# Head products, reciprocal transposes and first scaling half a unit apart at each batch's end, in a fused attention and mixture-of-experts kernel

## The chip, the cores and the metric

The kernel runs on one core of a Trainium2 chip. The core has TensorE for matmuls, VectorE, ScalarE and GpSimd (POOL) for everything elementwise, and SyncE (SP) for issuing DMAs. The metric is the device time of one execution in microseconds; lower is better.

## The reference

Three stages in a row: attention with capped scores over 4 batches, 12 heads, 448 positions and a head size of 64; a dense layer with a softmax gate and a layer norm over the 1792 tokens; and a layer of 8 experts that sends each token to one of them.

```python
scores = scale * np.matmul(q, k.transpose(0, 1, 3, 2))
scores = cap * np.tanh(scores / cap)
attn = np.exp(scores - max);  attn = attn / (attn.sum(-1) + 1e-09)
x = attn @ v                                   # then heads side by side: 1792 x 768
h = x @ w_in;  solu = h * softmax(h)
ln = (solu - mu) / np.sqrt(var + 1e-06) * g_ln
x = ln @ w_out                                 # then: top expert of 8, out = gate * relu(x @ w1) @ w2
```

## The kernel before

Heads are worked on in pairs, six pairs `p` to a batch `b`. Each pair is two halves, `cp` 0 and 1. In a half the scores of a pair are multiplied (tiles `sc`), ScalarE makes tanh and exp of them (tiles `e`), VectorE and POOL add the exponentials up (tiles `es`), and in the first half the pair before is multiplied with `v` (tile `av`) and copied to `X`. The row sums of all heads of a batch gather in one PSUM tile `S`. The scores are not divided at once: `X` is scaled when the batch is complete.

That scaling is what this document is about. It happens in two functions. `a_fin1` (lines 731 to 746) copies `S` to `ssb` on ScalarE, multiplies it with `comb` so that each head's sum stands in a column (line 737, the head products, tile `sum`), makes reciprocals on VectorE (lines 739 to 742, tile `rr`), transposes them on TensorE (line 744, the reciprocals' transposes) and copies them to `rh` on ScalarE and VectorE (745, 746). `a_fin2(b, q)` (748 to 757) spreads `rh` over the rows of two head pairs with two matmuls (line 751, tile `rb`) and scales that third of `X` on VectorE (line 753, the scaling); for batches 0 and 2 it copies the last columns to `tail`.

Between the attention's steps TensorE does the dense layer of the batches that are complete. Its steps stand in a list, `msteps`, and `fill(n)` takes as many from it as the pace allows: `h` (three matmuls each for `x @ w_in`), `lt` (transposes), `y` (three matmuls each for `ln @ w_out`). This is the filler. `fill` is called three times in a half, with 1, 0.7 and 1.3 points. When a batch has been scaled, `push_tile` adds the steps of its 128-token tiles, and `pace` sets the rate so that they last for a given number of points.

TensorE's instructions stand in the order in which the program writes them. The instructions of the other engines are put in order by a scheduler. All tiles on PSUM that the dense layer and the scores use (`sc`, `sum`, `rb`, `h`, `lt`, `y`) come from one pool of three buffers.

Which half the parts of the scaling stand in is given by `FIN`. Before, `finish(b - 1, u)` is called at the end of each half with `u = 2 * p + cp`; `FIN = (0, 1, 2, 2)` puts `a_fin1` at the end of the first half behind a batch, the first third of the scaling at the end of the second half, and the two other thirds and the push at the end of the third. The last batch is finished behind the loop, where `TAIL` says how many steps of the filler are left when each third comes.

Of the kernel before, what the change touches and what calls it, by code (L numbers as in the profile page):

```python
# [20 lines left out]
B, H, S, D = 4, 12, 448, 64  # L21
# [3 lines left out]
NP = H // 2  # L25
# [14 lines left out]
EARLY = 10  # L40
EDVE = ((0, 2), (0, 2, 3, 5, 7))
LTR = (2, 3, 4, 5, 7)
TAIL = (12, 12, 10)
NS = NK * len(KINDS)
NG = COL0["T"]
STATIC = [("D", 0), ("H", 0), ("D", 1), ("F", 0), ("H", 1)]
# [12 lines left out]
LSEP = (10, 12)  # L59
TRP = (4, 0, 0)  # L60
TRO = 1
FIN = (0, 1, 2, 2)
LEFT = (6, 6, 4)
RHA = 1
BIN = 0
# [17 lines left out]
def attn_moe_kernel(ctx, tc, qt, kt, vv, cap, w_in, w_out, g_ln, ids, w_gate, mbias, w1, w2, out):  # L83
# [334 lines left out]
    def atile(nm):  # L418
        return psA.tile([P, 2, 512], F32, tag="A", name=nm)

    def btile(nm):
        return psS.tile([P, 512], F32, tag="B", name=nm)
# [79 lines left out]
    def xtile(b):  # L502
        if b not in X:
            X[b] = xp.tile([P, NP, S], F32, tag="X", name=f"X{b}")
        return X[b]
# [99 lines left out]
    def direct(b, p):  # L605
        return b * NP + p < DIRECT

    def plain(b, p):
        return b * NP + p < PLAIN
# [25 lines left out]
    def a_split(b, p, js=(0, 1)):  # L635
        if plain(b, p):
            return
        k, q = raws[b, p]
        spl.setdefault((b, p), [])
        n = b * NP + p  # L640
        for j in js:
            kh = ap_.tile([P, S], F32R, tag="kh", name=f"kh{b}_{p}_{j}", bufs=3)
            kl = ap_.tile([P, S], F32R, tag="kl", name=f"kl{b}_{p}_{j}", bufs=3)
            qs = ap_.tile([P, S], F32R, tag="qs", name=f"qs{b}_{p}_{j}", bufs=3)
            (act.copy if n in KHA else dve.tensor_copy)(kh, k[j])  # L645
            (act.copy if n in QSA else dve.tensor_copy)(qs, q[j])
            dve.tensor_sub(qs[64:128], q[j][64:128], qs[64:128])
            (pool if n in KLP else dve).tensor_sub(kl, k[j], kh)  # L648
            spl[b, p].append((kh, kl, qs))
# [23 lines left out]
    def a_esp(b, p, cp):  # L673
        if direct(b, p) or not plain(b, p):
            return
        for j in range(2):
            if cp == 0:
                est[b, p, j] = ap_.tile([CK, S], F32, tag="es", name=f"es{b}_{p}_{j}", bufs=5)
                dve.tensor_add(est[b, p, j], et[b, p, j, 0], et[b, p, j, 1])
            else:  # L680
                dve.tensor_add(est[b, p, j], est[b, p, j], et[b, p, j, 2])
                dve.tensor_add(est[b, p, j], est[b, p, j], et[b, p, j, 3])
# [22 lines left out]
    def a_av(b, p, chunks=range(4)):  # L705

        if 0 in chunks:
            avt[b, p] = btile(f"av{b}_{p}")
            if p == 0:
                spt[b] = psS.tile([P, 512], F32, tag="S", name=f"S{b}")  # L710
        o, v = avt[b, p], vt[b, p]
        for c in chunks:
            for j in range(2):
                pe.matmul(o[64 * j:64 * j + 64, :S], v[:, c, 64 * j:64 * j + 64], et[b, p, j, c],  # L714
                          start=(c == 0), stop=(c == 3))
        if direct(b, p):
            for c in chunks:
                for j in range(2):
                    g = 2 * j + c % 2
                    pe.matmul(spt[b][32 * g:32 * g + 32, :S], zone[:, 31 - p:63 - p], et[b, p, j, c],  # L720
                              start=(p == 0 and c < 2), stop=(p == NP - 1 and c > 1))
        elif p % 2 and 3 in chunks:
            for j in range(2):
                for i in range(2):
                    g, pp = 2 * j + i, p - 1 + i
                    pe.matmul(spt[b][32 * g:32 * g + 32, :S], zone[:, 31 - pp:63 - pp], est[b, pp, j],
                              start=(p == 1), stop=(p == NP - 1))
        if 3 in chunks:
            (dve.tensor_copy if b * NP + p in XCD else act.copy)(xtile(b)[:, p, :], o[:, :S])

    def a_fin1(b):
        ssb = ap_.tile([P, S], F32, tag="es", name=f"ssb{b}", bufs=5)
        act.copy(ssb, spt[b][:, :S])
        po = atile(f"sum{b}")
        ps = po[:CK, 0, :4 * H].rearrange("p (c h) -> p c h", h=H)
        for c in range(4):
            pe.matmul(ps[:, c, :], ssb[:, c * CK:(c + 1) * CK], comb, start=True, stop=True)
        r = ap_.tile([CK, 4, HR], F32, tag="es", name=f"rr{b}", bufs=5)
        dve.memset(r, 0.0)
        dve.tensor_scalar(r[:, :, :H], ps, epsv[:CK], None, op0=ALU.add)  # L740
        dve.reciprocal(r[:, :, :H], r[:, :, :H])
        dve.tensor_copy(r[:, :, 32:], r[:, :, :H])
        for c in range(4):
            pe.transpose(po[:HR, 1, c * CK:(c + 1) * CK], r[:, c, :], ident[:CK, :CK])
        (act if RHA else dve).__getattribute__("copy" if RHA else "tensor_copy")(rh[:HR], po[:HR, 1, :S])
        dve.tensor_sub(rh[32:HR], po[32:HR, 1, :S], rh[32:HR])

    def a_fin2(b, q):
        po = atile(f"rb{b}_{q}")
        for i in range(2):  # L750
            pe.matmul(po[:, i, :S], sel[:, 2 * q + i, :], rh, start=True, stop=True)
        x = X[b][:, 2 * q:2 * q + 2, :]
        dve.tensor_mul(x, x, po[:, :, :S])
        if (b + 1) * S % P:
            if q == 0:
                tail[b] = xp.tile([P, NP, (b + 1) * S % P], F32, tag="tail", name=f"tail{b}", bufs=1)
            dve.tensor_copy(tail[b][:, 2 * q:2 * q + 2, :], x[:, :, S - (b + 1) * S % P:])
# [13 lines left out]
    msteps, drained = [], set()  # L771
# [29 lines left out]
    def pace(points):  # L801
        rate[0] = sum(c for c, _ in msteps) / points + 0.01
        rate[1] = 0.0

    def fill(n):
        rate[1] += n * rate[0]
        while msteps and rate[1] > 0:
            c, f = msteps.pop(0)
            f()
            rate[1] -= c  # L810

    def finish(b, u):

        if u == FIN[0]:
            a_fin1(b)
        for q in range(3):
            if u == FIN[q + 1]:
                a_fin2(b, q)
        if u == FIN[3]:
            for t in range(NTILE):  # L820
                if (t * P + P - 1) // S == b:
                    push_tile(t)
            pace(3 * (2 * NP - FIN[3]) + LEFT[b])

    with tc.manual_schedule(engines={mybir.EngineType.PE}):
        a_load(*pairs[0])
        a_split(*pairs[0])
        v_load(*pairs[0])
        a_load(*pairs[1])
        for _ in range(4):  # L830
            conv_load()
        setup_tables(xp)
        for n, (b, p) in enumerate(pairs):
            for cp in range(2):
                if plain(b, p):
                    a_scp(b, p, cp)
                else:
                    a_sc(b, p, 0, cp)
                if cp == 0 and n:
                    a_av(*pairs[n - 1], chunks=(2, 3) if plain(*pairs[n - 1]) else range(4))  # L840
                elif cp and plain(b, p):
                    a_av(b, p, chunks=(0, 1))
                deferred(0)
                fill(FW[0])
                a_esp(b, p, cp)
                if cp == 0 and n + 1 < len(pairs):
                    a_split(*pairs[n + 1], js=(0,))
                if not plain(b, p):
                    a_sc(b, p, 1, cp)
                fill(FW[1])  # L850
                if cp == 1 and n + 1 < len(pairs):
                    a_split(*pairs[n + 1], js=(1,))
                if cp == 1 and n + 2 < len(pairs):
                    a_load(*pairs[n + 2])
                if cp == 0 and n + 1 < len(pairs):
                    v_load(*pairs[n + 1])
                fill(FW[2])
                while convs and (not convs[0][0] or CUS[crate[0]] <= 2 * n + cp):
                    crate[0] += convs[0][0]
                    convs.pop(0)[1]()  # L860
                if b > 0:
                    finish(b - 1, 2 * p + cp)
        a_av(B - 1, NP - 1)
        fill(2)
        a_fin1(B - 1)
        t = (B - 1) * S // P - 1
        msteps.insert(len(msteps) - TRO, (W[1], lambda: m_tr(t)))
        push_y(t)
        drained.add(t)
        rate[1] = 0.0  # L870
        for q in range(3):
            while len(msteps) > TAIL[q]:
                msteps.pop(0)[1]()
            a_fin2(B - 1, q)
        fill(1e9)
    ap_.release()
    psS.release()
    rt = tc.alloc_tile_pool(name="rt", bufs=1, side="right", reuse_waits="tile")
# [534 lines left out]
```

## Time and profile before

| what | value |
|---|---|
| median of 3 runs | 789.97 us (789.9 to 790.86) |
| the profiled execution's own time | 788.29 us |
| its span, first to last instruction | 786.6 us |
| mean granted clock of TensorE | 0.980 |
| TensorE busy | 737.2 us, 94% |
| VectorE busy | 452.6 us, 58% |
| ScalarE busy | 393.7 us, 50% |
| POOL busy | 209.8 us, 27% |

The attention with the dense layer between it takes the first 410 us or so, and the experts the rest. Busy shares are means over the whole span; what one stage waits for is read from that stage.

### The profile page before, as it was taken

Reading aid. Unit: us, or ns where it says so; the run is one execution under the profiler, and the core shown is the slowest. Engines: PE = TensorE matmul, PEld = TensorE weight load, DVE = VectorE, ACT = ScalarE, POOL = GpSimd, SP = SyncE. Lnnn points to the kernel's source line nnn. Section 1 sums busy time; section 2 is a strip of 40 time slices with the busy share of each in tenths; the row PEclk is TensorE's granted clock in tenths of the full one; section 3 lists DMA queues with packets and bytes.
Section 4 is the critical chain, followed back from the end, with each engine's and each line's share of the span. In section 5 each row is a group of like instructions: output and inputs, shape, how many; then the busy total and the mean of one; then the engine's idle time right before and its main releaser. Section 6 shows DMA issues by size and latency. Waiting matters only on the chain.

```text
span 786.6 us, 11389 instructions
## 1 busy us (share of the span) xinstructions
PE 737.2 (94%) x4150; PEld 576.3 (73%) x4150; DVE 452.6 (58%) x833; ACT 393.7 (50%) x541; POOL 209.8 (27%) x285
## 2 busy tenths in 40 slices
PE   6889899998999998999999999899999999999993
PEld 2234456776677777676868799889879988799982
DVE  5987767767656665665444745747246163463630
ACT  5987656774656554556641223525136162553530
POOL 4222015352343351336432213540300211002010
PEclk9999999999999999999999999999999999999997
DMA  9856202231313221122000402476938459574620
GB/s 299 284 178 168 90 19 82 67 109 54 102 36 102 79 69 60 57 69 79 13 21 20 142 21 91 128 277 218 362 135 251 147 173 379 199 254 166 211 79 23
DMA packets 39060, 104.50 MB, mean 133 GB/s; under 512 B 6439, under 2 KB 16689, under 8 KB 38994
## 3 DMA queue, kind: packets, MB, share of 16 engines
q1 hardware_dynamic: 32466, 74.26, 29.0%
q0 software_dynamic: 6528, 29.42, 10.8%
q8 instruction: 34, 0.56, 0.3%
q14 instruction: 32, 0.26, 0.1%
HBM read 92.58 MB, written 11.27 MB: 132 GB/s over the span
## 4 chain that ended last, share of the span: by engine, by line
PE 78%; DVE 7%; issue 6%; ACT 3%; DMA 3%; POOL 1%; SPq 0%; POOLq 0%; DVEq 0%; ACTq 0%
PE av L714 8%; PE h L536 5%; PE y L586 5%; PE h L538 5%; PE y L588 5%; PE y L587 5%; PE h L537 5%; PE sc L689 3%; PE sc L690 3%; PE poD L1160 3%; PE poD L1161 3%; PE poD L1162 3%; PE phD L1091 3%; PE phD L1092 3%; PE phD L1093 3%
## 5 line engine op out<-in xcount | busy, mean ns | idle before, releaser
L692 ACT ACTIVATE e<-sc,sc 112x896 f32<-112x896 f32 x64 | 64.6, 1009 | 83.4 <-PE sc L690 81.2
L714 PE MATMUL av<-e,v 112*64 112x448 f32 x384 | 82.0, 560 | 3.1 <-ACT e L669 2.3
L586 PE MATMUL y<-wouh,lh 128*128 128x388 f32 x224 | 77.4, 345 | 2.2 <-ACT lh L576 1.9
L588 PE MATMUL y<-wouh,ll 128*128 128x388 f32 x224 | 76.4, 341 | 0.3 <-DVE ll L577 0.2
L587 PE MATMUL y<-woul,lh 128*128 128x388 f32 x224 | 76.2, 340 | 0.0
L536 PE MATMUL h<-winh,xh 128*128 128x512 f32 x168 | 69.3, 413 | 0.1
L538 PE MATMUL h<-winh,xl 128*128 128x512 f32 x168 | 66.8, 398 | 0.9 <-POOL xl L524 0.5
L693 ACT ACTIVATE e<-e,cap_t 112x896 f32<-112x896 f32 x64 | 66.9, 1045 | 1.5
L537 PE MATMUL h<-winl,xh 128*128 128x512 f32 x168 | 66.5, 396 | 0.0
L714 PEld LDWEIGHTS av<-e,v 112*64 112x64 f32 x384 | 24.9, 140 | 53.1 <-issue 38.4
L689 PE MATMUL sc<-qs,kh 128*112 128x448 f32 x128 | 48.2, 377 | 2.3 <-DVE u L548 1.3
L701 POOL TENSOR_TENSOR es<-es,e 112x448 f32<-112x448 f32 x32 | 40.8, 1276 | 34.1 <-DVE es L700 33.5
L586 PEld LDWEIGHTS y<-wouh,lh 128*128 128x128 f32 x224 | 42.4, 189 | 8.4 <-issue 4.3
L648 POOL TENSOR_TENSOR kl<-kr,kh 128x448 fp32r<-128x448 f32 x22 | 28.3, 1288 | 75.3 <-DVE kh L645 44.9
L690 PE MATMUL sc<-qs,kl 128*112 128x448 f32 x128 | 47.7, 372 | 0.0
L1037 DVE TENSOR_TENSOR wl_H<-raw_H,wh_H 128x768 fp32r<-128x768 f32 (+1 forms) x28 | 29.2, 1068 | 29.4 <-ACT wh_H L1036 29.3
L1037 DVE TENSOR_TENSOR wl_D<-raw_D,wh_D 128x768 fp32r<-128x768 f32 (+1 forms) x28 | 29.8, 1071 | 24.6 <-ACT wh_D L1036 24.0
L588 PEld LDWEIGHTS y<-wouh,ll 128*128 128x128 f32 x224 | 42.2, 188 | 1.1 <-DVE ll L577 1.0
L587 PEld LDWEIGHTS y<-woul,lh 128*128 128x128 f32 x224 | 42.3, 189 | 0.9
L1160 PE MATMUL poD<-wh_D,hhD 128*128 128x384 f32 x128 | 43.0, 336 | 0.0
L1162 PE MATMUL poD<-wh_D,hlD 128*128 128x384 f32 x128 | 42.8, 334 | 0.0
L1161 PE MATMUL poD<-wl_D,hhD 128*128 128x384 f32 x128 | 42.8, 334 | 0.0
(382 smaller groups left out, 1769.0 us busy)
## 6 DMA issues: line engine op xcount, KB each, us to landing
kr<-in_kt_dram SPq DMA_DIRECT2D x64, 112.0 KB, 2.5
qr<-in_qt_dram SPq DMA_DIRECT2D x64, 112.0 KB, 2.6
rawc<-in_w_in_dram POOLq DMA_DIRECT2D x12, 512.0 KB, 5.8
rawc<-in_w_out_dram POOLq DMA_DIRECT2D x16, 384.0 KB, 3.8
raw_D<-in_w_dram SPq DMA_DIRECT2D x12, 512.0 KB, 3.9
wr_T<-in_w_dram SPq DMA_DIRECT2D x16, 384.0 KB, 5.7
raw_D<-in_w_dram SPq DMA_DIRECT2D x16, 384.0 KB, 4.5
wr_T<-in_w_dram SPq DMA_DIRECT2D x12, 512.0 KB, 9.0
```

Of the source, the lines that this page charges most:

```text
L536: pe.matmul(o, s["xh"][d], winh[d][:, c], start=(d == 0), stop=False)
L537: pe.matmul(o, s["xh"][d], winl[d][:, c], start=False, stop=False)
L538: pe.matmul(o, s["xl"][d], winh[d][:, c], start=False, stop=(d == ND - 1))
L586: pe.matmul(o, s["lh"][f], wouh[f][:, c], start=(f == 0), stop=False)
L587: pe.matmul(o, s["lh"][f], woul[f][:, c], start=False, stop=False)
L588: pe.matmul(o, s["ll"][f], wouh[f][:, c], start=False, stop=(f == NF - 1))
L689: pe.matmul(ps[:CK, c, :S], kh[:, k0:k0 + CK], qs, start=True, stop=False)
L690: pe.matmul(ps[:CK, c, :S], kl[:, k0:k0 + CK], qs, start=False, stop=True)
L693: act.activation(e, e, AF.Exp, scale=cap_t[:CK])
L714: pe.matmul(o[64 * j:64 * j + 64, :S], v[:, c, 64 * j:64 * j + 64], et[b, p, j, c], start=(c == 0), stop=(c == 3))
L1160: pe.matmul(p, hh[:, f, o], wh[:, c], start=(f == 0), stop=False)
L1161: pe.matmul(p, hh[:, f, o], wl[:, c], start=False, stop=False)
```

## The change

`a_fin1` becomes three functions. `a_ssb` copies `S` as soon as the batch's last attention output is there. `a_sums` makes the head products and the reciprocals, and `a_recip` transposes them, into a PSUM tile of its own (`rt`). `finish` is called twice in a half, behind the first `fill` and at its end, with `u` counting half units. `FIN = (2, 3, 4, 5, 5)` puts the products in the middle of the second half behind a batch, the transposes at its end, the first third of the scaling in the middle of the third half, and the two other thirds and the push at its end, which is where they were. The pace is set over three points less. Behind the loop, products and transposes are separate too, with a new first entry of `TAIL` between them.

```diff
-TAIL = (12, 12, 10)
+TAIL = (14, 12, 12, 10)
-FIN = (0, 1, 2, 2)
+FIN = (2, 3, 4, 5, 5)
...
+            if p == NP - 1:
+                a_ssb(b)
+
+    sums = {}
+
+    def a_ssb(b):
         ssb = ap_.tile([P, S], F32, tag="es", name=f"ssb{b}", bufs=5)
         act.copy(ssb, spt[b][:, :S])
-        po = atile(f"sum{b}")
+        sums[b] = ssb
+
+    def a_sums(b):
+        ssb, po = sums[b], atile(f"sum{b}")
...
+        sums[b] = r
+
+    def a_recip(b):
+        r, po = sums.pop(b), atile(f"rt{b}")
         for c in range(4):
             pe.transpose(po[:HR, 1, c * CK:(c + 1) * CK], r[:, c, :], ident[:CK, :CK])
...
         if u == FIN[0]:
-            a_fin1(b)
+            a_sums(b)
+        if u == FIN[1]:
+            a_recip(b)
         for q in range(3):
-            if u == FIN[q + 1]:
+            if u == FIN[q + 2]:
                 a_fin2(b, q)
-        if u == FIN[3]:
+        if u == FIN[4]:
...
-            pace(3 * (2 * NP - FIN[3]) + LEFT[b])
+            pace(3 * (2 * NP - (FIN[4] + 1) // 2) + LEFT[b])
...
                 fill(FW[0])
+                if b > 0:
+                    finish(b - 1, 4 * p + 2 * cp)
...
                 if b > 0:
-                    finish(b - 1, 2 * p + cp)
+                    finish(b - 1, 4 * p + 2 * cp + 1)
         a_av(B - 1, NP - 1)
         fill(2)
-        a_fin1(B - 1)
+        a_sums(B - 1)
+        while len(msteps) > TAIL[0]:
+            msteps.pop(0)[1]()
+        a_recip(B - 1)
...
-            while len(msteps) > TAIL[q]:
+            while len(msteps) > TAIL[q + 1]:
```

How the instructions stand. First TensorE, at the end of batch 1. The last number of a name is a running number; `y_1654` and `y_1612` are the filler's tile at that place.

Before:

```order
L588 MATMUL y_1654<-wouh_133,ll_1542 128x388
L737 MATMUL sum_1666<-comb,ssb_1664 112x12 x4
L744 MATMUL sum_1666<-ident,rr_1671 44x112 x4
L689 MATMUL sc_0_0_1_1682<-qs_0_0_1493,kh_0_0_1491 112x448
L690 MATMUL sc_0_0_1_1682<-qs_0_0_1493,kl_0_0_1492 112x448
```

After, TensorE around the head products and then around the transposes:

```order
L586 MATMUL y_1612<-wouh_134,lh_1530 128x388
L587 MATMUL y_1612<-woul_142,lh_1530 128x388
L588 MATMUL y_1612<-wouh_134,ll_1531 128x388
L744 MATMUL sum_1704<-comb,ssb_1643 112x12 x4
L689 MATMUL sc_0_1_1_1714<-qs_0_1_1575,kh_0_1_1573 112x448
L690 MATMUL sc_0_1_1_1714<-qs_0_1_1575,kl_0_1_1574 112x448
```

```order
L586 MATMUL y_1612<-wouh_138,lh_1530 128x388
L587 MATMUL y_1612<-woul_146,lh_1530 128x388
L588 MATMUL y_1612<-wouh_138,ll_1531 128x388
L755 MATMUL rt_1762<-ident,rr_1709 44x112 x4
L689 MATMUL sc_1_0_0_1769<-qs_1_0_1653,kh_1_0_1651 112x448
L690 MATMUL sc_1_0_0_1769<-qs_1_0_1653,kl_1_0_1652 112x448
```

The transposes stood directly behind the products; now a score tile and 12 `y` matmuls stand between them, and one score tile more stands ahead of the products. (In the changed file the products are line 744, the transposes 755, the `rb` matmuls 762.)

Second TensorE, at the two later thirds of the same batch's scaling, in the third half. Before (18 `y` matmuls stand ahead of these rows in the half):

```order
L588 MATMUL y_1654<-wouh_138,ll_1542 128x388
L751 MATMUL rb_1_1812<-rh,sel 128x448 x2
L751 MATMUL rb_2_1816<-rh,sel 128x448 x2
L689 MATMUL sc_1_0_1_1820<-qs_1_0_1617,kh_1_0_1615 112x448
L690 MATMUL sc_1_0_1_1820<-qs_1_0_1617,kl_1_0_1616 112x448
```

After:

```order
L714 MATMUL av_0_1779<-e_0_1_1_1719,v_0_1536 64x448
L762 MATMUL rb_0_1791<-rh,sel 128x448 x2
L689 MATMUL sc_1_1_0_1802<-qs_1_1_1732,kh_1_1_1730 112x448
L690 MATMUL sc_1_1_0_1802<-qs_1_1_1732,kl_1_1_1731 112x448
...
L762 MATMUL rb_1_1814<-rh,sel 128x448 x2
L762 MATMUL rb_2_1818<-rh,sel 128x448 x2
L689 MATMUL sc_1_0_1_1822<-qs_1_0_1653,kh_1_0_1651 112x448
```

The first third, `rb_0`, has come into this half, and no `y` matmul is left in it: the filler's list is empty from the transposes to the push.

Third VectorE at the same place, where line 753 (764 after) is the scaling, 698 a sum of exponentials and 729 the copy of `av` to `X`. Before:

```order
L753 TENSOR_TENSOR X_959<-X_959,rb_0_1742 128x896
L698 TENSOR_TENSOR es_1_0_1754<-e_1_0_0_1751 112x448
L729 COPY X_1766<-av_0_1756 128x448
L590 SCALAR_TENSOR_TENSOR lg<-y_1654,sm_1301,bias_t 128x8
L592 TENSOR_REDUCE nmx<-lg 128x1
L753 TENSOR_TENSOR X_959<-X_959,rb_1_1812 128x896
L698 TENSOR_TENSOR es_1_1_1792<-e_1_1_0_1789 112x448
L753 TENSOR_TENSOR X_959<-X_959,rb_2_1816 128x896
L645 CAST kh_2_1_1868<-kr_2_1_1727 128x448
```

After:

```order
L698 TENSOR_TENSOR es_1_0_1777<-e_1_0_0_1774 112x448
L729 COPY X_1789<-av_0_1779 128x448
L764 TENSOR_TENSOR X_954<-X_954,rb_0_1791 128x896
L764 TENSOR_TENSOR X_954<-X_954,rb_1_1814 128x896
L764 TENSOR_TENSOR X_954<-X_954,rb_2_1818 128x896
L698 TENSOR_TENSOR es_1_1_1810<-e_1_1_0_1807 112x448
L645 CAST kh_2_1_1873<-kr_2_1_1743 128x448
```

The three scalings, which had other work between them, stand in a row.

## Rows read from the trace of the kernel before

**Rows 1.** The page: busy us of each engine; the chain that ended last, by engine.

```profile
PE 737.2 (94%) x4150; PEld 576.3 (73%) x4150; DVE 452.6 (58%) x833; ACT 393.7 (50%) x541; POOL 209.8 (27%) x285
...
PE 78%; DVE 7%; issue 6%; ACT 3%; DMA 3%; POOL 1%; SPq 0%; POOLq 0%; DVEq 0%; ACTq 0%
```

**Rows 2.** Waits of TensorE: us in total, times, longest.

```profile
PE sum L744 <- DVE rr L742: 6.4, 4, 2.1
...
PE sum L737 <- ACT ssb L733: 1.5, 1, 1.5
```

**Rows 3.** Timeline, end of batch 1: start, us, engine, line, [idle before <- releaser].

```profile
184.87 0.95 PE L737 MATMUL sum<-comb,ssb 128*112 128x12 f32 x8 [1.51 <-ACT ssb L733]
...
186.05 1.27 DVE L551 BATCH_NORM_STATS2 bn<-u 128x6 f32<-128x512 f32 x2
...
187.95 0.94 PE L744 MATMUL sum<-ident,rr 112*44 112x112 f32 x4 [2.13 <-DVE rr L742]
```

**Rows 4.** Timeline, TensorE's transposes at the ends of batches 0, 2 and 3.

```profile
91.25 0.56 PE L744 MATMUL sum<-ident,rr 112*44 112x112 f32 x4 [1.69 <-DVE rr L742]
...
304.02 0.94 PE L744 MATMUL sum<-ident,rr 112*44 112x112 f32 x4 [1.49 <-DVE rr L742]
...
410.47 0.56 PE L744 MATMUL sum<-ident,rr 112*44 112x112 f32 x4 [1.07 <-DVE rr L742]
```

**Rows 5.** Stretches: length, busy us per engine, granted clock (1.00 full), DMA, GB/s.

```profile
92.00:96.00 4.00, 4.00 (x14) 1.18 (x14) 3.07 (x7) 3.26 (x4) 0.00 (x0) 0.57 0.04 7
102.00:106.00 4.00, 4.00 (x13) 1.43 (x14) 1.52 (x3) 2.00 (x3) 0.00 (x0) 0.57 0.01 4
188.00:192.00 4.00, 4.00 (x16) 3.68 (x17) 3.00 (x5) 2.07 (x3) 2.75 (x5) 0.59 0.00 0
304.00:308.00 4.00, 3.98 (x14) 3.35 (x15) 2.38 (x4) 2.00 (x3) 1.17 (x1) 0.58 0.00 0
314.00:330.00 16.00, 13.67 (x66) 9.37 (x66) 8.60 (x17) 7.34 (x12) 5.97 (x10) 1.00 0.15 46
```

**Rows 6.** Timeline, weight conversion near the end of batch 0, TensorE.

```profile
100.08 0.52 PE L486 MATMUL pt<-ident,to 128*128 128x128 f32 x3 [1.23 <-DVE to L428]
```

**Rows 7.** Timeline, TensorE's waits around the push of batches 1 and 2.

```profile
205.35 0.45 PE L689 MATMUL sc<-qs,kh 128*112 128x448 f32 x1 [0.56 <-ACT ys L597]
...
207.35 0.50 PE L538 MATMUL h<-winh,xl 128*128 128x512 f32 x1 [0.49 <-POOL xl L524]
...
315.45 0.43 PE L689 MATMUL sc<-qs,kh 128*112 128x448 f32 x1 [1.31 <-DVE u L548]
...
321.21 0.44 PE L586 MATMUL y<-wouh,lh 128*128 128x388 f32 x1 [0.32 <-DVE lg L590]
...
327.54 0.45 PE L689 MATMUL sc<-qs,kh 128*112 128x448 f32 x1 [0.18 <-ACT ys L597]
...
329.86 0.50 PE L538 MATMUL h<-winh,xl 128*128 128x512 f32 x1 [0.45 <-DVE xl L524]
```

**Rows 8.** Timeline: durations at the push; last a stretch with VectorE's four split instructions.

```profile
202.21 0.34 PE L586 MATMUL y<-wouh,lh 128*128 128x388 f32 x1
...
203.81 0.97 PE L751 MATMUL rb<-rh,sel 128*128 128x448 f32 x4
...
204.41 1.09 DVE L753 TENSOR_TENSOR X<-X,rb 128x896 f32<-128x896 f32 x1
205.42 0.62 DVE L698 TENSOR_TENSOR es<-e 112x448 f32<-112x448 f32 x1
...
316.58 1.01 ACT L692 ACTIVATE e<-sc,sc 112x896 f32<-112x896 f32 x1 [2.53 <-PE sc L690]
...
319.69 0.62 DVE L729 COPY X<-av 128x448 f32<-128x448 f32 x1 [0.98 <-PE av L714]
...
328.10 0.51 ACT L523 CAST xh<-X 128x384 fp32r<-128x384 f32 x1 [0.19 <-DVE X L753]
...
206.95:209.05 2.10, 1.70 (x7) 1.41 (x8) 2.07 (x5) 1.79 (x3) 0.55 (x2) 1.00 0.47 189
```

More of the change, by code (lines that the diff above doesn't have):

```diff
@@ L729, in a_av @@
             (dve.tensor_copy if b * NP + p in XCD else act.copy)(xtile(b)[:, p, :], o[:, :S])
-    def a_fin1(b):
+            if p == NP - 1:
+                a_ssb(b)
+    sums = {}
+    def a_ssb(b):
         ssb = ap_.tile([P, S], F32, tag="es", name=f"ssb{b}", bufs=5)
         act.copy(ssb, spt[b][:, :S])
-        po = atile(f"sum{b}")
+        sums[b] = ssb
+    def a_sums(b):
+        ssb, po = sums[b], atile(f"sum{b}")
         ps = po[:CK, 0, :4 * H].rearrange("p (c h) -> p c h", h=H)
```

## Prediction

> **What bounds the kernel now.** I read the page first: TensorE is busy for 94% of the span, and on the chain of work that ended last it holds 78% [rows 1]. So a microsecond counts where TensorE stands still, and work that only moves within its queue costs nothing. Next the list of who TensorE waited for. It puts 6.4 us, in four waits, on the reciprocals' transposes (line 744), and 1.5 us, in one, on the head products (line 737) [rows 2]. Four waits are four seams, the places where a batch ends. I call them seam 1 (batch 0) to seam 4 (batch 3, behind the loop).
>
> Then the timeline at each seam. At seam 2 the products start after 1.51 us of idle behind ScalarE's copy `ssb`, and the transposes after another 2.13 us, while VectorE took 1.27 us of batch statistics between the reciprocal's steps [rows 3]. Seams 1, 3 and 4 have 1.69, 1.49 and 1.07 us in front of the transposes [rows 4]. Last the stretches with their granted clock. [...] One such fall loses 4 x (1 - 0.58) = 1.7 us of full-speed work. Seam 1 has a second fall, 102 to 106 us, behind a wait of 1.23 us for the weight conversion [rows 5, 6].
>
> **The change part by part.** No arithmetic is added. Each seam has the same 8 matmul records of head products, 4 transposes and 6 scaling products, one more PSUM tile (`rt`), and the same DMAs in the same order on SP and POOL's queues; the store of a finished tile (`m_out`) goes to POOL's queue a few microseconds sooner, with its filler, and nothing waits for it there.
>
> *Removed at seams 1 to 3.* The copy `ssb` now follows the last attention output at once, and half a unit or more of matmuls stands between it and the products; between products and transposes stand four score matmuls and 12 to 21 `y` matmuls. Nine `y` matmuls take 1.6 us (202.21 to 203.81) [rows 8], so 12 of them and four score matmuls, at about the same length, cover 2.8 us at seam 2, and 21 and four 4.4 us at seam 3. The chain on VectorE that they have to cover was 2.13 us at its worst [rows 3], so it is hidden. At seam 2 it removes 1.51 + 2.13 = 3.64 us and a fall of the clock (1.7), at seam 3 1.49 and a fall (1.7), at seam 1 1.69 and at best both falls (3.4). If the cover were gone, these same waits would come back.
>
> *Not removed at seam 4.* In the written order the transposes follow the products directly there, because no more than 14 steps are left when the new loop is reached. The 1.07 us stays, without a fall, as before: 0.
>
> *Given back.* Half a unit later than before the first scaling falls into the same half pair as the second and the third, and since the pace is set over 33 points instead of 36, the filler runs out half a unit sooner. So from the transposes on, TensorE has no `y` matmul until the next tile's first `h`; before, 18 stood there at seam 2 and 30 at seam 3. What was a pause for VectorE is gone. I work it through from the end of `av` with the durations of [rows 8] and the written order.
>
> Seam 2: VectorE has a sum of exponentials first, whose exponential ScalarE ends about 0.5 us late (an estimate: it has a copy, the store's scaling, tanh and exp in front, about 1 us each but the copy). The sum takes 0.62, the copy of `X` 0.62, the first scaling 1.09, so the scaling is done at 2.9. TensorE does `rb_0`, a score tile and `rb_1` by 1.7 (0.45 + 0.8 + 0.45), and `rb_2` needs one of three PSUM buffers, that of `rb_0`: 1.25 us idle. `rb_2` and a score tile go to 4.2; the second scaling ends at 4.0 and ScalarE's split, of half a tile, at 4.4 or a little later (0.25 idle); POOL's half of the split comes as late behind it as before (0.49). New idle 2.0 us. In the same place there were 0.56 + 0.49 = 1.05 us before [rows 7]. Net given back 0.95.
>
> Seam 3: no sum stands in front, so the first scaling ends at 1.8 and `rb_2` waits 0.15; but ScalarE's split stands behind the tanh and exp of two score tiles (4 x 1.0), and takes 0.51 itself. Counted from `av`'s end the first of these four can start at 0.3 to 0.4 (the scores before it), so `h` starts at 4.9 where TensorE was ready at 3.1 (1.8 idle), and VectorE's half of the split comes as late behind it as before (0.45). New idle 2.4, against 1.31 + 0.32 + 0.18 + 0.45 = 2.26 before [rows 7]: 0.14 given back. An idle of 1.8 us in one piece is longer than the 1.49 that a fall followed, and that 1.31 was not followed by one; by the nearest row I count a fall here, 1.7.
>
> Seam 1: 1.69 goes and one of two falls (1.7). The second `po` group waits for a copy that now stands behind `ssb`, another copy of about 0.5; the transposes of the next block reach VectorE's conversion sooner than it is ready (1.23 becomes about 1.9 [rows 6]); and the two score tiles of the push wait for the first and the second scaling, which VectorE does in a row with two sums between them (1.09, and 0.62 x 2, against 0.5 us of `rb` in front: some 0.6 + 1.5). That is 3.3 given back against 3.4: 0. The bounds are -1.69 - 3.4 = -5.1 (both falls gone, nothing given back) and 3.3 - 1.69 = +1.6 (no fall saved).
>
> **A rule weighed.** Rows first: at seams 1 to 3 the fall followed one idle of 1.5 to 2.1 us, and short idles of 0.2 to 0.45 us, three of them between 321 and 330 us, were not followed by one [rows 5, 7]. [...]
>
> **The sum.** Seam 1: 0. Seam 2: -3.64 - 1.7 + 0.95 = -4.4. Seam 3: -1.49 - 1.7 + 0.14 + 1.7 = -1.4. Seam 4: 0. Together -5.8 us. The profiled execution took 788.29 us around a span of 786.6, so it would take 782.5; it lies 1.7 below the median of the runs, 789.97, and the forecast is for the median: **784.2 us**. Behind the loop nothing changes in the order, and the weights' loads follow TensorE's progress, so the gain is carried to the end.
>
> **The rivals.** *All of it.* Nothing is given back, because the other engines are early enough in the filler-free half. Then -(1.69 + 3.4) - 5.34 - 3.19 = -13.6, at most; halfway from the forecast -9.7: 780.3 us. For it speaks that the idles at the push of seam 3 were partly for the filler's own tiles (1.31 for `u`, 0.32 for `lg`), which are now done earlier; against it that three scalings of 1.09 us stand in a row.
>
> *Returned.* The clock falls at seam 2 as well (+1.7) and neither fall at seam 1 is saved (+1.7): -2.4; with another microsecond of idle -1.4 us: 788.6, which can't be told from no change (0.2% is 1.6 us, about what a measurement of this kernel tells).
>
> *Slower.* VectorE becomes the bound of the push half: if the next pair's four casts and differences (2.1 us together) and a sum (0.62) come ahead of the second scaling at seams 1 to 3 [rows 8], each idles 2.7 us more, and the clock falls at all of them: 3 x 2.7 + 2 x 1.7 = 11.5 on top of -5.8, which is +5.7: 795.7 us. It decides where idle and falls take 5.8 us more than I worked out, about 2 us at each seam. Against it: in the order of the instructions the three scalings stand ahead of those casts at seam 2.
>
> **How the numbers follow.** Forecast (gain of 2 to 8 us) 0.56; all of it 0.16; returned 0.17; slower 0.11. Faster by over 0.2%: 0.56 + 0.16 = 0.72; within: 0.17; slower: 0.11. The likeliest case's own range is 781.5 to 788. The range, 778.5 to 789.5, leaves out the slower case and the far end of the first rival, less than 2 in 10 together.
>
> **What would show it.** In the profile after: the transposes' line waits only at seam 4, about 1 us, and the head products' line nowhere. The clock around 188 and 302 us no longer falls at the transposes; if it falls, it does at the first `h` of tile 7, some 20 us later. `rb` waits for VectorE's scaling and the first `h` for the split, 1 to 2 us each. Seam 1 keeps a wait for the conversion and one fall. Wrong would be: a fall behind the push at seam 2, or idle in front of the scores behind `rb_2` of more than 3 us.

## The result

The changed kernel takes **780.68 us** (median of 6 runs, 779.59 to 784.63); the kernel before, run beside it, 789.93 (6 runs, 787.79 to 791.53). The ratio is **0.9877**, 95% interval 0.9849 to 0.9906: faster by 1.2%, 9.3 us by the medians. A second set of executions of the same kernel, on another occasion, gave 0.9894 (0.9848 to 0.9939). The forecast, 784.2, had the right sign and a gain that was too small; the first rival ("all of it", 780.3) came nearer. The profiled execution has a span of 778.4 us where [rows 1]'s kernel had 786.6: 8.2 us less, and the rest of this text accounts for these.

First the list of who TensorE waited for in the changed kernel (us in total, times, longest):

```profile
PE pt L486 <- DVE to L428: 4.1, 2, 2.0
...
PE sc L664 <- DVE X L764: 1.6, 2, 1.2
PE h L536 <- ACT xh L523: 1.5, 1, 1.5
PE rb L762 <- DVE X L764: 1.2, 1, 1.2
PE rt L755 <- DVE rr L749: 1.2, 1, 1.2
```

The 6.4 us of the transposes and the 1.5 us of the products [rows 2] have become 1.2 us in one wait, at seam 4. New are waits for VectorE's scaling (line 764: `sc` at seam 1, `rb` at seam 2) and one for ScalarE's split (`h`, seam 3). The timeline of TensorE at seams 1 to 4, products (744), transposes (755) and what waits:

```profile
97.78 0.88 PE L486 MATMUL pt<-ident,to 128*128 128x128 f32 x3 [2.04 <-DVE to L428]
...
108.36 1.01 PE L664 MATMUL sc<-qr,kr 64*112 64x448 f32 x4 [0.43 <-DVE X L764]
...
110.57 1.01 PE L664 MATMUL sc<-qr,kr 64*112 64x448 f32 x4 [1.20 <-DVE X L764]
...
188.53 0.86 PE L744 MATMUL sum<-comb,ssb 128*112 128x12 f32 x8
...
192.25 0.55 PE L755 MATMUL rt<-ident,rr 112*44 112x112 f32 x4
...
199.83 0.68 PE L762 MATMUL rb<-rh,sel 128*128 128x448 f32 x2 [1.23 <-DVE X L764]
...
320.27 0.50 PE L536 MATMUL h<-winh,xh 128*128 128x512 f32 x1 [1.50 <-ACT xh L523]
...
406.76 0.54 PE L755 MATMUL rt<-ident,rr 112*44 112x112 f32 x4 [1.16 <-DVE rr L749]
```

At seam 2 neither the products nor the transposes have a bracket now; before, they had 1.51 and 2.13 us [rows 3]. The granted clock, by stretches (length, busy us, clock, DMA, GB/s):

```profile
188.00:192.00 4.00, 4.00 (x27) 1.00 0.26 74
98.00:104.00 6.00, 6.00 (x25) 0.50 0.02 4
200.00:212.00 12.00, 12.00 (x58) 1.00 0.27 78
290.00:330.00 40.00, 37.90 (x196) 1.00 0.27 79
```

Where the clock stood at 0.59 and 0.58 before, at 188 and 304 us [rows 5], it is at 1.00. Of the seams only seam 1 keeps a stretch at half of that, 0.50 from 98 to 104 us.

Where the time came from is read from one landmark, the first `h` behind each push (at seam 4 the first behind the scalings, in the loop of the routed part). By then both kernels have done the same work. Times are starts in the timelines; a stretch is the difference of two landmarks.

| stretch, us | before | after | difference | forecast |
|---|---|---|---|---|
| start to `h` at seam 1 | 111.88 | 113.16 | +1.3 | 0 |
| to `h` at seam 2 | 94.36 | 88.06 | -6.3 | -4.4 |
| to `h` at seam 3 | 122.43 | 119.05 | -3.4 | -1.4 |
| to `h` behind seam 4 | 101.81 | 101.62 | -0.2 | 0 |
| to the end of the span | 356.1 | 356.5 | +0.4 | 0 |

Seams 2 and 3 each gave 2 us more than forecast. At seam 3, 1.7 of them are the fall of the clock that was forecast behind the `h` and did not come in this profile; by these landmarks it would stand in the stretch to seam 4 (-3.1 and +1.7 in place of -1.4 and 0). The +1.3 of the start can't be put down to seam 1 from these two profiles alone, as the next section shows.

### The profile page after: what moved, and what is told of

It is laid out like the page before. It is cut to its first block, busy times and chain, and to the rows that moved or that the text cites. A ratio compares the mean times of both kernels' runs of the same rounds, so it can differ in the third digit from the quotient of the medians.

```text
span 778.4 us, 11381 instructions
## 1 busy us (share of the span) xinstructions
PE 733.1 (94%) x4150; PEld 575.0 (74%) x4150; DVE 452.9 (58%) x833; ACT 392.1 (50%) x541; POOL 209.5 (27%) x285
## 4 chain that ended last, share of the span: by engine, by line
PE 79%; DVE 7%; issue 6%; ACT 3%; DMA 3%; POOL 1%; SPq 0%; POOLq 0%; ACTq 0%; DVEq 0%
PE av L714 7%; PE h L536 5%; PE h L538 5%; PE h L537 5%; PE y L586 5%; PE y L588 5%; PE y L587 5%; PE sc L689 3%; PE sc L690 3%; PE poD L1178 3%; PE poD L1180 3%; PE poD L1179 3%; PE phD L1109 3%; PE phD L1110 3%; PE phD L1111 3%
```

## The experiments

Two theories stood at the start. *Chain*: the gain is VectorE's chain (epsilon, reciprocal, copy) taken out from in front of the transposes, with the falls of the clock behind it. *Pace*: the gain is that the filler is spread over 33 points instead of 36, so that its own waits near the push are gone. Each experiment gives its ratio to the kernel before, run beside it, and the three stretches between the landmarks (seam 1 to 2, 2 to 3, 3 to 4) of one profile. The stretch behind the loop differs by up to 4 us between profiles with the same order there (356.1 before, 356.5 after, 360.2 in one below), and the start by up to 6.5 us (112.2 us in five apart, 118.7 in five apart, pace 30, whose orders are the same up to there), so a reading of a seam goes by the stretches.

| kernel | ratio (95%) | stretches, us | their sum |
|---|---|---|---|
| before | 1 | 94.4, 122.4, 101.8 | 318.6 |
| after | 0.9877 (0.9849 to 0.9906) | 88.1, 119.1, 101.6 | 308.7 |
| after, again | 0.9894 (0.9848 to 0.9939) | 88.1, 119.1, 102.9 | 310.0 |
| together | 1.0066 (1.0035 to 1.0097) | 90.5, 125.3, 103.2 | 318.9 |
| late copy | 0.9911 (0.9876 to 0.9946) | 88.0, 120.1, 103.2 | 311.3 |
| pace 36 | 0.9963 (0.9938 to 0.9989) | 90.0, 122.1, 101.3 | 313.4 |
| pace 36, shared tile | 0.9946 (0.9925 to 0.9968) | 90.0, 120.5, 101.3 | 311.7 |
| before, pace 33 | 1.0057 (1.0035 to 1.0080) | 89.8, 126.5, 101.7 | 318.0 |
| seam 1 as before | 0.9895 (0.9860 to 0.9930) | 88.0, 119.1, 103.2 | 310.3 |
| half earlier | 0.9937 (0.9913 to 0.9961) | 88.5, 121.4, 103.3 | 313.2 |
| five apart | 0.9857 (0.9825 to 0.9889) | 86.9, 117.8, 102.0 | 306.8 |
| five apart, split first | 0.9829 (0.9796 to 0.9862) | 86.9, 117.8, 100.9 | 305.7 |
| five apart, tail | 0.9878 (0.9859 to 0.9897) | 87.0, 117.8, 100.9 | 305.7 |
| five apart, pace 30 | 1.0071 (1.0044 to 1.0097) | 100.2, 118.9, 103.4 | 322.4 |

**Together.** Products and transposes side by side again, all else as after.

```diff
-FIN = (2, 3, 4, 5, 5)
+FIN = (2, 2, 4, 5, 5)
```

> Against the kernel after (780.7 us): products and transposes stand side by side again, in the middle of the second half, everything else as after. Theory 'chain' (the gain is VectorE's chain taken out from in front of the transposes, with the clock falls behind it): idles of 1.5 to 2.1 us are back in front of the transposes at seams 1 to 3, and a fall of the clock of 1.7 us behind them at seams 2 and 3: 2.1 + 1.7 + 1.5 + 1.7 + up to 1.7 = 7 to 8.7 us more, 786 to 789.5. Rival 'pace' (the gain is that the filler is done half a unit sooner, so that its own waits at the push are gone) and rival 'copy' (the gain is the early copy of the sums): 780 to 782.

It is slower than the kernel before, and by more than *chain* expected. The timeline of TensorE:

```profile
97.12 0.54 PE L755 MATMUL rt<-ident,rr 112*44 112x112 f32 x4 [1.91 <-DVE rr L749]
...
194.90 0.91 PE L755 MATMUL rt<-ident,rr 112*44 112x112 f32 x4 [1.40 <-DVE rr L749]
...
210.04 0.49 PE L538 MATMUL h<-winh,xl 128*128 128x512 f32 x1 [1.57 <-POOL xl L524]
...
317.31 0.54 PE L755 MATMUL rt<-ident,rr 112*44 112x112 f32 x4 [2.94 <-DVE rr L749]
...
333.01 0.50 PE L536 MATMUL h<-winh,xh 128*128 128x512 f32 x1 [1.50 <-ACT xh L523]
```

The stretches behind the last two, with the clock as the third figure from the end:

```profile
316.00:320.00 4.00, 2.69 (x11) 0.72 0.21 61
334.00:338.00 4.00, 4.00 (x12) 0.60 0.30 85
```

The transposes wait at all three seams; at seam 3 for 2.94 us where it was 1.49 before [rows 4]. The waits of the filler-free push (1.57 and 1.50) come on top. So at this pace the split is needed, and *pace* alone doesn't carry the gain.

**Late copy.** `a_ssb` is called in `a_sums` again.

```diff
             (dve.tensor_copy if b * NP + p in XCD else act.copy)(xtile(b)[:, p, :], o[:, :S])
-            if p == NP - 1:
-                a_ssb(b)
...
     def a_sums(b):
+        a_ssb(b)
```

> The kernel after with the copy of the sums back in the unit of the head products. Theory 'chain': the products wait 1 to 1.5 us for the copy at seam 2, perhaps at seams 1 and 3, with a fall of the clock behind one of them: 781.5 to 785. Rival 'copy' (the early copy is most of the gain): 787 to 790. Rival 'pace': no change, 780 to 781.5.

The products don't wait (186.60 in the timeline, without a bracket), and the stretch to seam 2 is 88.0 as after. So the median of 784.38 us lies in the range of *chain* without the wait that *chain* named. Nor does the old place of the products need the early copy at the new pace: in the kernel before with pace 33, below, the copy is late, and the products don't wait. The copy's place does show at seam 3, where the filler waits for `lg`:

```profile
303.80 0.45 PE L586 MATMUL y<-wouh,lh 128*128 128x388 f32 x1 [1.46 <-DVE lg L590]
```

After, this wait is 0.43 us (304.74). In VectorE's order a sum of exponentials and another instruction have come ahead of `lg`, and the second stretch is longer by the same 1.0 us (120.1 for 119.1). The third stretch is 1.6 us longer than after's (103.2 for 101.6), as in the other profiles where the clock fell behind the `h` wait of seam 3 (102.9 to 103.3); that is taken up below. The ratio's interval overlaps that of after, so the runs don't settle what the copy is worth in the whole.

**Pace 36.** The filler as before.

```diff
-            pace(3 * (2 * NP - (FIN[4] + 1) // 2) + LEFT[b])
+            pace(3 * (2 * NP - FIN[4] // 2) + LEFT[b])
```

> The kernel after with the filler spread over as many points as before (36, 36 and 34), so that 18 and 30 y matmuls stand between the transposes and the next tile's first h again. Rival 'pace' (the gain is the sooner end of the filler): 787 to 790. Theory 'chain': the y matmuls cover the waits at the push (1.2 us at seam 2, 1.5 at seam 3) but bring back the filler's own (0.56 + 0.49 at seam 2, 1.31 + 0.32 at seam 3): 779 to 782.5.

The ratio is on the side of *pace*: split without it, the change would have gained 0.4%. At seam 2 the split alone does most of its work all the same: the first stretch is 90.0, where before has 94.4 and after 88.1. The timeline of TensorE shows what comes back, and one wait that is worse than before:

```profile
138.79 1.06 PE L568 MATMUL lt<-ident,u 128*128 128x128 f32 x8 [0.73 <-DVE u L553]
...
143.65 0.43 PE L689 MATMUL sc<-qs,kh 128*112 128x448 f32 x1 [0.18 <-DVE ll L577]
...
192.54 0.54 PE L755 MATMUL rt<-ident,rr 112*44 112x112 f32 x4 [1.02 <-DVE rr L749]
...
310.81 0.43 PE L689 MATMUL sc<-qs,kh 128*112 128x448 f32 x1 [2.48 <-DVE sm L556]
```

And the clock (0.72) around the last:

```profile
310.00:316.00 6.00, 5.19 (x18) 0.72 0.22 60
```

The first two are the filler's own, in the middle of the batch; the kernel before has them to the hundredth (0.73 at 136.75 and 0.18 at 141.61), the one after not at all. The last is the scores' wait for VectorE's work on an `h` tile, presumably for that tile's PSUM buffer; it was 1.31 us before [rows 7] and is now 2.48 with a fall behind it.

**Before, pace 33.** The other half alone: the kernel before, with the points of after.

```diff
-            pace(3 * (2 * NP - FIN[3]) + LEFT[b])
+            pace(3 * (2 * NP - FIN[3] - 1) + LEFT[b])
```

> The kernel before with the filler over 33, 33 and 31 points, nothing else. Theory 'both' (the sooner filler and the split gain only together): the filler's waits behind the pushes go (0.73 + 0.18 at 137 to 142 us, 1.31 + 0.32 + 0.18 at seam 3), but the transposes still wait 1.5 to 2.1 us at seams 1 to 3 with their falls of the clock, and the push has new waits of 1 to 1.5 us at seams 2 and 3: ratio to before 0.997 to 1.003. Rival 'pace': 0.988 to 0.992. Rival 'chain' (the pace does nothing): 1.000 with the old waits.

No gain; the ratio lies even above the range of *both*. The stretches' sum is that of before within 0.6 us; 4 us of this profile's loss lie behind the loop (360.2 for 356.1), where the order is unchanged. Most of these are two waits of the experts' matmuls (line 1091; 1.32 us at 552.90 and 2.37 at 652.83, where before has one of 1.31) and a fall behind the second (0.97 over the 60 us from 611.79, where before has 1.00). Why they are longer, and whether they are in every run, isn't known, so a part of the ratio stays unexplained. At the seams, timeline of TensorE:

```profile
189.26 0.56 PE L744 MATMUL sum<-ident,rr 112*44 112x112 f32 x4 [1.07 <-DVE rr L742]
...
203.62 0.50 PE L536 MATMUL h<-winh,xh 128*128 128x512 f32 x1 [1.34 <-ACT xh L523]
...
205.63 0.50 PE L538 MATMUL h<-winh,xl 128*128 128x512 f32 x1 [1.27 <-POOL xl L524]
...
310.99 0.56 PE L744 MATMUL sum<-ident,rr 112*44 112x112 f32 x4 [3.14 <-DVE rr L742]
```

At 137 to 142 us nothing waits any more. But the sooner filler puts another tile's statistics on VectorE just where the chain runs at seam 3 (3.14 us), and leaves the push without cover. At seam 2 the pace alone does much: the products don't wait, the transposes wait 1.07 us for 2.13, and the first stretch is 89.8 for 94.4. What it gains there it loses at seam 3 (126.5 for 122.4). Pace alone +0.6%, split alone -0.4%, both -1.2%: at seam 3 each takes away the wait that the other makes worse (the transposes' 3.14 us, the scores' 2.48).

**Pace 36, shared tile.** The transposes go into the products' PSUM tile, as before the change.

```diff
-        sums[b] = r
+        sums[b] = r, po
...
-        r, po = sums.pop(b), atile(f"rt{b}")
+        r, po = sums.pop(b)
```

> The kernel after with the old pace (36, 36, 34), and the transposes again in the PSUM tile of the products, which is then held over the half unit between them. Theory 'buffer' (at the old pace the scores wait 2.48 us for the statistics at seam 3 since the extra PSUM tile of the transposes takes a buffer that an h tile in flight still holds): that wait falls to the 1.3 us of before or less, with no fall of the clock behind it, and the ratio is 0.991 to 0.994. Rival (the tile held longer is as bad as an extra one, or the wait is for VectorE's own queue): the wait stays over 2 us and the ratio is 0.996 to 0.999.

```profile
308.72 0.45 PE L586 MATMUL y<-wouh,lh 128*128 128x388 f32 x1 [0.74 <-ACT e L692]
...
314.07 0.43 PE L689 MATMUL sc<-qs,kh 128*112 128x448 f32 x1 [1.52 <-DVE sm L556]
```

The wait falls from 2.48 to 1.52 us, and no clock falls behind it (1.00 from 314 to 324 us). But in front of it stands a wait of 0.74 us that pace 36 doesn't have, so TensorE idles 2.26 us in all for 2.48: holding the tile longer costs nearly what the extra tile did, as the rival said. The second stretch is shorter by 1.6 us (120.5 for 122.1), about the fall that is missing in this profile. The ratio, 0.9946, has an interval that covers both theories.

**After, again.** The same kernel in other executions.

> The kernel after, unchanged, in other executions. Theory 'chance' (an idle of about 1.5 us lies at the edge, so the same wait is followed by a fall of the clock in some executions and not in others): the waits are those of the first profile within 0.1 us, but the first h at seam 3 (1.5 us idle, no fall in the first profile) may be followed by a fall; the runs lie 1.7 us or twice that apart, 779 to 785. Theory 'place' (what stands in front of the idle decides): no fall behind that h here either.

The timeline at seam 3:

```profile
321.95 0.68 PE L536 MATMUL h<-winh,xh 128*128 128x512 f32 x1 [1.50 <-ACT xh L523]
```

The stretch behind it, with the clock at 0.57:

```profile
322.00:326.00 4.00, 4.00 (x11) 0.57 0.19 56
```

The wait is the same to the hundredth; in the first profile the clock stayed at 1.00, here it falls. *Chance* holds.

**Seam 1 as before.** At batch 0 alone the copy, products and transposes at the end of the first half of the second pair, as before.

```diff
+FINS = {0: (1, 1, 3, 5, 5), 1: (2, 3, 4, 5, 5)}
...
-            if p == NP - 1:
+            if p == NP - 1 and b:
                 a_ssb(b)
...
     def a_sums(b):
+        if b == 0:
+            a_ssb(b)
...
     def finish(b, u):
+        FIN = FINS.get(b, FINS[1])
```

> The kernel after, but at seam 1 alone the order of before (copy, products and transposes together at the end of the first half of the second pair, first scaling half a pair later). Theory 'chain': seam 1 cost the change 1.2 us (waits of 4.4 us for 3.2 us), which come back, while the waits and clocks of seams 2 to 4 stay: the first h at seam 1 about 1.2 us sooner, the whole 778.5 to 780. Rival (the start that comes sooner is lost again at a wait for a load or behind seam 1): 780 to 782.

The waits of before are back there: 0.28, 1.79 and 1.24 us, together 3.3, instead of 4.4. From the second `pt` group of the seam (88.43) to the first `h` (114.18) it takes 25.75 us, before 25.68, after 26.75, after again 27.49: 1.0 to 1.7 us that the change lost at seam 1. The whole doesn't show it: 0.9895 against 0.9877 and 0.9894, and 783.17 us, outside both ranges; in this profile the clock also fell behind the `h` of seam 3 (0.50 from 324 to 326 us).

**Half earlier.** Products, transposes and first scaling each half a unit sooner.

```diff
-FIN = (2, 3, 4, 5, 5)
+FIN = (1, 2, 3, 5, 5)
```

> The kernel after with products, transposes and the first scaling each half a unit sooner (still half units apart), the other two scalings and the push where they were; the pace is the same. Theory 'chain': the first scaling is done before the push, so that the third rb's wait at seam 2 (1.2 us) and the scores' waits at seam 1 (0.4 + 1.2) go; at seam 2 only four score and six y matmuls stand between products and transposes, some 1.9 us by the durations after, against a chain of 2.1 us: a wait of 0.2 to 1 us there. Together 777.5 to 780. Rival (the order of the scalings isn't what TensorE waits for, and the split and the next tile's scores wait just as long): 780 to 782.

The waits of `rb` (1.23) and of seam 1's scores are gone, but `h` waits 1.34 at seam 2 and 1.50 at seam 3, each with a fall (the `h` matmuls behind go from 0.40 us to 0.63 and 0.60): 0.9937, worse than the rival's range. ScalarE at seam 3:

```profile
318.00 1.01 ACT L692 ACTIVATE e<-sc,sc 112x896 f32<-112x896 f32 x1 [2.02 <-PE sc L690]
319.04 1.05 ACT L693 ACTIVATE e<-e,cap_t 112x896 f32<-112x896 f32 x1
320.15 1.01 ACT L692 ACTIVATE e<-sc,sc 112x896 f32<-112x896 f32 x1
321.06 0.50 ACT L523 CAST xh<-X 128x384 fp32r<-128x384 f32 x1
```

The split `xh` stands behind three activations of the score tiles.

**Five apart**, and the same with the split's first half issued at the push and nine `y` matmuls between products and transposes at seam 4 (**split first**).

```diff
-FIN = (2, 3, 4, 5, 5)
+FIN = (1, 2, 3, 4, 5)
```

```diff
-TAIL = (14, 12, 12, 10)
+TAIL = (3, 12, 12, 10)
...
-        msteps.append((0.0, lambda: m_split(t)))
+        first = not msteps
+        if first:
+            m_split(t, (0,))
+        msteps.append((0.0, lambda: m_split(t, (1,) if first else (0, 1))))
```

> The kernel after with all five steps half units apart: products at the end of the first half, transposes, the three scalings each half a unit later, the third with the push at the old place. Theory 'ScalarE queue' (the first h waits because ScalarE's split stands in its queue behind tanh and exp of the score tile that comes with the push): h still waits 1.3 to 1.5 us at seams 2 and 3, as where only the first scaling was moved, so 781 to 785. Rival 'scaling' (h waits since the second scaling is late): h waits under 0.5 us, 777 to 780.

> As the kernel with five steps half units apart; in addition the first half of the next tile's split is issued at the push itself, ahead of the tanh and exp of the next score tiles on ScalarE, and at seam 4 nine y matmuls stand between products and transposes. Theory 'ScalarE queue': the first h waits under 0.5 us at seams 2 and 3 instead of 1.3 to 1.5, the transposes at seam 4 don't wait (1.16), and with one or two falls of the clock less the time is 776 to 780. Rival (the split waits at the head of ScalarE's queue for the scaling and holds up the tanh, so that the wait turns up at the scores or at av): 781 to 785.

Five apart (780.49 us) already has no wait of 0.15 us or more at the first `h` of seams 2 and 3, so *ScalarE queue*, as I had put it, fell: the split needs no place of its own. With the second scaling half a unit sooner it comes two activations sooner in ScalarE's order by itself. The early split adds nothing at seams 2 and 3 (86.9 and 117.8 in both).

**Five apart, tail** is five apart with the `TAIL` line alone.

> The kernel with the five steps half units apart, and at seam 4 nine y matmuls between products and transposes; no change of the split. Theory 'scaling' (with the second scaling sooner the split comes two activations sooner in ScalarE's order, and h needn't wait): h doesn't wait at seams 2 and 3, the transposes don't at seam 4 (1.17 gone), and the ratio is 0.982 to 0.986. Rival (the early split was what made the faster kernel): 0.985 to 0.988 with a wait of over 0.5 us at h.

ScalarE and TensorE at seam 3, and the transposes at seam 4:

```profile
315.32 1.01 ACT L692 ACTIVATE e<-sc,sc 112x896 f32<-112x896 f32 x1 [2.43 <-PE sc L690]
316.22 0.50 ACT L523 CAST xh<-X 128x384 fp32r<-128x384 f32 x1
...
316.78 0.51 PE L536 MATMUL h<-winh,xh 128*128 128x512 f32 x1
...
404.00 0.55 PE L755 MATMUL rt<-ident,rr 112*44 112x112 f32 x4
```

The split follows the first tanh, `h` doesn't wait, and seam 4's 1.16 us is gone. By the stretches this is 3.1 us better than after, but the ratio, 0.9878, is that of after and lies in the rival's range, though the waits are as *scaling* said. With the early split (0.9829) all four runs, 777.74 to 779.63 us, lie below all four of after again, 780.47 to 786.22, taken on the same occasion.

**Five apart, pace 30.** The filler over 30, 30 and 28 points.

```diff
-            pace(3 * (2 * NP - (FIN[4] + 1) // 2) + LEFT[b])
+            pace(3 * (2 * NP - 4) + LEFT[b])
```

> The kernel with the five steps half units apart, and the filler over 30, 30 and 28 points, so that only four score matmuls (0.8 us) stand between products and transposes at seams 2 and 3. Theory 'cover': the chain of about 2.1 us at seam 2 and 1.5 at seam 3 is no longer covered, the transposes wait 0.7 to 1.4 us there, and the scores and h behind them wait too: 3 to 7 us more than with the points of after, ratio 0.989 to 0.995. Rival 'pace' (the sooner the filler ends, the better): 0.980 to 0.985.

*Pace* falls, and *cover* was too mild. The timeline of TensorE:

```profile
141.81 1.97 PE L568 MATMUL lt<-ident,u 128*128 128x128 f32 x8 [4.24 <-DVE u L553]
...
208.80 0.64 PE L755 MATMUL rt<-ident,rr 112*44 112x112 f32 x4 [2.54 <-DVE rr L749]
```

The transposes, with four scores as their only cover, wait 2.54 us; and the filler, pulled forward once more, runs into its own tile's statistics (4.24 us). So the gain of 33 points does not mean that sooner is better: 36 and 30 points each have waits that 33 has not.

## Why the prediction was right in sign and too small in size

**Removed at seams 2 and 3: right.** The 3.64 and 1.49 us and a fall at each seam are gone. But the reason named first, the early copy, was not needed for this (late copy): the products don't wait for a late copy either, at their new place or, at the new pace, at the old one. And at seam 2 the split was not the only way: the pace alone takes away 1.51 + 1.06 = 2.57 of the 3.64 us and the fall behind them (the clock is 1.00 from 188 to 204 us).

**"Given back", seam 2 (0.95 us): the step that failed.** I took the sooner end of the filler for a cost only: "What was a pause for VectorE is gone." What it gave back is 1.23 - (0.56 + 0.49) = 0.18 us: the wait at `rb_2` was sized rightly (1.25), but the 0.25 and 0.49 us behind it, for the split, did not come. Before and after, ScalarE's and POOL's half of the split with what stands in front on POOL:

```profile
205.63 0.34 ACT L523 CAST xh<-X 128x192 fp32r<-128x192 f32 x1
206.02 0.65 POOL L600 DMA_DIRECT2D ysc<-ys  x1 [8.19 <-ACT xh L523]
206.70 0.60 POOL L524 TENSOR_TENSOR xl<-X,xh 128x192 fp32r<-128x192 f32 x1
```

```profile
200.81 0.35 ACT L523 CAST xh<-X 128x192 fp32r<-128x192 f32 x1 [0.50 <-DVE X L764]
201.25 0.59 POOL L524 TENSOR_TENSOR xl<-X,xh 128x192 fp32r<-128x192 f32 x1 [3.77 <-ACT xh L523]
```

ScalarE's half ends at 201.16, about as forecast, but `rb_2` and its score tile keep TensorE until 201.22. POOL's half starts 0.1 us behind it; before, POOL first issued the store of a finished tile (line 600) and started 0.7 us behind. The store now comes sooner, with its filler, and I had written that "nothing waits for it there". And the sooner filler removed two waits that I had not listed, 0.73 and 0.18 us at 137 to 142 us, in the middle of the batch, where I had not looked for a consequence of the pace. -3.64 - 1.7 + 0.18 - 0.91 = -6.1; measured -6.3. Of this sum 0.49 lies behind the landmark, in the next stretch; the first stretch itself has 5.1 us of waits before and 1.2 after, and a fall less, which is -5.6. The 0.7 us left are in no wait that the timeline shows, and stay open. Pace 36 brings the two waits back, before with pace 33 takes them away.

**Seam 3 (0.14 given back, and a fall of 1.7 counted).** New idle is 0.43 + 1.50 + 0.15 = 2.1 us against 2.26 [rows 7], for the cause named (the split behind tanh and exp): forecast 2.4. That the size came out is in part luck: the first tanh started at 316.65, some 1.5 us behind `av` (to 315.20) and not 0.3 to 0.4, but three activations stood in front of the split (319.71) and not four. The fall behind the `h` was absent in the profile after and present in the second profile of the same kernel. In the profile without it the term is -3.4, with it about 1.2 to 1.6 us less (third stretch 102.9 to 103.2 for 101.6). I had counted as certain what happens in some executions.

**Seam 1 (0): too good.** Waits of 0.72 + 2.04 + 0.43 + 1.20 = 4.4 us stand where 0.28 + 1.69 + 1.23 = 3.2 stood, and no stretch at half speed was saved: one longer one (0.50 from 98 to 104 us) took the place of two (0.57 each [rows 5]). The given-back 3.3 us were near (0.5, 0.7 and 2.1 forecast; 0.4, 0.8 and 1.6 measured); the fall "saved" was not.

**Seam 4 (0): right**, 1.16 us for 1.07.

**The rivals.** *Slower* needed VectorE's casts ahead of the second scaling: no such wait came. Of *Returned* one half came, no fall saved at seam 1, and the other did not: behind the push of seam 2, with its wait of 1.23 us, the clock is 1.00 from 200 to 212 us. Each fall between seams 1 and 4 in these profiles followed an idle of 1.3 us or more, two of them with a second idle close by (1.51 and 2.13 us before; 1.34 and 1.27 us in before, pace 33). None of the profiles shows there a fall behind small idles alone. *All of it* named the right thing without pricing it: "the idles at the push of seam 3 were partly for the filler's own tiles (1.31 for `u`, 0.32 for `lg`), which are now done earlier".

That the split and the pace belong together is shown by four kernels: sums of stretches 318.6 (neither), 318.0 (pace), 313.4 (split), 308.7 (both). At seam 2 either alone gives most of the gain (89.8 and 90.0 for 94.4; both 88.1); at seam 3 only both do (126.5 and 122.1 for 122.4; both 119.1). Open stays why the kernel before at pace 33 is slower by 0.6% in its runs with the same sum, and how much of the difference between after and the five-apart kernels is real in the whole.

## What to carry to other kernels

A constant that spreads filler work moves that work's own waits in the whole batch, not only where it ends: list every wait of the filler before and ask of each whether it still stands. Before splitting a chain, look at what else its engine has to do between the halves and behind them; here the split alone gained 0.4%, the sooner filler alone nothing, and both 1.2%. And where a step waits for its turn on another engine, as the split did behind three activations on ScalarE, look at which of its inputs is ready last before giving it a place of its own: here an earlier input moved it by itself.

## What the runs showed of the hardware

The clock did not answer the same idle alike in every profile. Over the 14 profiles, between the first `h` of seam 1 and that of seam 4, I counted TensorE's idles of 0.9 us or more. Of 23 idles of 0.91 to 1.23 us none was followed by a fall (behind the 1.23 us of after the clock is 1.00 from 200 to 212 us); at seam 1, ahead of this stretch, one of 1.23 us was [rows 5, 6]. All six places with an idle of over 2 us were: 2.13 in before (0.59 from 188 to 192 us [rows 3, 5]), 2.48 in pace 36 (0.72, 310 to 316), 2.54 and 4.24 in five apart, pace 30 (0.72, 208 to 214; 0.57, 140 to 148), 2.94 in together (0.72, 316 to 320) and 3.14 in before, pace 33 (0.57, 312 to 316).

Between lie the uncertain ones. The `h` wait of 1.50 us at seam 3 stands in seven profiles and was followed by a fall in five: after, again (0.57, 322 to 326 us), together (0.60, 334 to 338), seam 1 as before (0.50, 324 to 326), half earlier (an `h` matmul of 0.60 us behind it) and late copy (its third stretch, 103.2 us, is as long as theirs). In after (1.00 up to 330 us) and in before, pace 33 (1.00, 330 to 336) it was not. Single idles of 1.31 us (before; 1.00 up to 330 us [rows 5, 7]), 1.41 (five apart, pace 30; 1.00, 330 to 338), 1.46 (late copy; the second stretch is longer by the wait alone), 1.52 (pace 36, shared tile; 1.00, 314 to 324) and 1.57 (together; the `h` matmuls behind take 0.39 to 0.40 us) were not followed by one, while others of 1.34 (half earlier; `h` matmuls of 0.63 us for 0.40), 1.40 (together; score matmuls of 0.57 us for 0.37) and 1.49 (before; 0.58, 304 to 308 [rows 4, 5]) were; once a fall came behind two idles, 1.34 and 1.27 us, 2 us apart (before, pace 33; 0.57, 206 to 210). What decides between them no profile here shows.

A single fall is worth 4 x (1 - 0.58) = 1.7 us of full-speed work [rows 5], and the third stretch was 1.2 to 1.7 us longer with it than without (102.9 to 103.3 for 101.6 and 101.7). So two executions of one kernel can lie that much apart, and a forecast should count such a fall by its odds.
